# A fused attention and gated MLP: token blocks of 768, 1024 and 512 in place of three of 768

## The chip, the cores and the metric

The kernel runs on one core of a Trainium2 chip. What counts is the time of one execution on the device, in microseconds, as the median of three runs.

## What is computed

Attention with a causal mask and a memory term, over 4 batches, 8 heads, 576 positions and head size 64, gives x of 2304 tokens by 512. A gated MLP follows, which is where the change lies:

```python
g = x @ w_gate            # 512 -> 1536
silu = g * (1.0 / (1.0 + np.exp(-g)))
val = x @ w_val
return silu * val @ w_out # 1536 -> 512
```

All of it is float32. A product in the MLP is made of three matmuls on operands that are split into a high and a low part (names ending in h and l): high x high, high x low, low x high.

## The kernel before

**Stages.** The attention runs first, up to about 183 us of the trace, and writes x to DRAM as xdh and xdl (high and low). The MLP then works on three blocks of tokens, which start at ORDER. d_ff is cut into 12 slices (f) of 128.

**Block 1** (tokens 0 to 767) goes slice by slice. For each slice its weights are decoded and split (third, operands), the up products made, and u, the gated product of 384-token halves, is multiplied with w_out at once into six PSUM banks (lower). The first three slices are plain (eight); from slice 3 on a slice is seven steps in the manner of Strassen (seven, chain), p1, p2, p6, p7, p5, p4, p3, numbered 0 to 6 here. Each step is six matmuls (product: two halves of the contraction, three of the high-low products), with a weight part of 128x128 stationary and N2 = 384 tokens moving. Steps alternate between two PSUM banks, so a bank must be read before the step after the next. Steps 2, 4, 5 and 6 add onto what their bank holds, after it has been read. After step 0 ACT copies to zp, after step 1 DVE adds it into zg, after 2 and 3 ACT copies to zh and zv, after 4 and 5 DVE adds to zv and zh, and after 6 DVE multiplies twice (use): zg and zh are then the two halves of u.

**Blocks 2 and 3** are computed only up to u, which goes to DRAM (udr) with its sums (mixed, tiles zs). During slices 6 to 11 of block 1 DVE makes the sums of x that the steps of blocks 2 and 3 need (sums, tiles xr, xt, xm for block 2 and yr, yt, ym for block 3), and ACT and DVE split them into the places of the strip xall or, for block 3, into tiles yp1h, yp1l and so on (high, low, spreads). After block 1 come solo passes: slice 11 of block 2, slice 10 of block 2, slice 10 of block 3, slice 11 of block 3. Then a paired loop takes slices 0 to 9, a step of block 2 and a step of block 3 in turn, each with its own two banks.

**The down phase** multiplies u with w_out, again in seven products, each over three chunks of d_ff for block 2 and then three for block 3 (chunks, 42 in all). A chunk has 128-token row tiles, six matmuls each, with 256 columns of w_out moving. Its operand is loaded six chunks ahead and split three chunks ahead (prep, LEAD). taken evacuates a finished product, and the last store ends the kernel.

**What sets the order.** Work on PE, ACT, DVE and GpSimd (POOL) goes out in the order in which the program text issues it (queued, whose line 92 is the line of nearly all rows). The lists plan[n] say what DVE and ACT do behind step n. An instruction waits in its queue for what it needs, and all that stands behind it on its engine waits too. Loads and stores are issued on SP's queue.

Lines that matter below: N2 and ORDER (27, 30), sums (773), product (809), chain (887), the plans of slices 6 to 11 (1002 to 1027), the solo passes (1045, 1073, 1085, 1110), the paired loop (1162), prep (1125), and the down phase (1199 to 1255).

## Time and profile before

| | |
|---|---|
| median of 3 runs | 590.47 us (589.98 to 590.79) |
| profiled execution, its own time | 590.32 us |
| span from the first to the last instruction in it | 588.5 us |
| PE busy | 579.0 us, 98% |
| DVE, ACT, POOL busy | 478.1, 391.9, 236.5 us |
| granted TensorE clock, mean | 0.997 |

The span is what lies between the first and the last instruction of the profiled execution; the 1.8 us beside it are around the program. A row of the timeline begins with the start in us from the span's start and the duration in us, then engine, line, operation, output <- inputs, sizes and how many such instructions were merged; brackets show the engine's idle time before it and what ended that. Matmuls are pipelined: a row of 0.34 us doesn't mean that the next starts after 0.34 us, so the distance between starts is what one costs. s and tr are PSUM banks, woh and wol the split down weights, th, tl, bh, bl the split up weights.

### The profile page before, as it was taken

What the parts mean: (1) busy time and instruction counts of PE and PEld (TensorE: products, weight loads), DVE (VectorE), ACT (ScalarE), POOL (GpSimd) and SP (SyncE); (2) the same over time, 40 slices, a digit from 0 to 9 for tenths busy, and PEclk for the clock granted to TensorE, in tenths of its full rate; (3) what the DMA queues carried; (4) which work ended last, traced back from release to release, by engine and by line L of the source; (5) the groups of instructions that cost most, each with busy time, mean ns of one, the idle gap of its engine ahead of it and who ended that gap; (6) DMA issues with size and microseconds to landing.
All of it is one profiled execution on the core that took longest, in us unless ns stands there. A gap on an engine that the chain in (4) does not pass through costs nothing.

```text
span 588.5 us, 11998 instructions
## 1 busy us (share of the span) xinstructions
PE 579.0 (98%) x4118; PEld 535.5 (91%) x4118; DVE 478.1 (81%) x1161; ACT 391.9 (67%) x895; POOL 236.5 (40%) x285
## 2 busy tenths in 40 slices
PE   6999999999999999999999999999999999999997
PEld 4888888878878999999999999999999999999997
DVE  7899999999988989899998778677777776985771
ACT  7898998998887578777844655444444446646741
POOL 6999999999975333433340002122220000000000
PEclk9999999999999999999999999999999999999999
DMA  8446856757417555699848587365475426998852
GB/s 252 144 141 189 282 157 200 251 170 219 171 64 278 200 176 187 209 311 280 267 163 301 163 284 224 135 215 189 178 249 215 138 111 201 310 402 279 266 194 80
DMA packets 66092, 124.26 MB, mean 211 GB/s; under 512 B 8304, under 2 KB 37360, under 8 KB 66032
## 3 DMA queue, kind: packets, MB, share of 16 engines
q1 hardware_dynamic: 65744, 123.21, 63.0%
q8 instruction: 32, 0.52, 0.4%
q10 hardware_dynamic: 288, 0.30, 0.1%
q14 instruction: 28, 0.23, 0.1%
HBM read 80.23 MB, written 43.25 MB: 210 GB/s over the span
## 4 chain that ended last, share of the span: by engine, by line
PE 94%; ACT 2%; DMA 1%; DVE 1%; POOL 1%; issue 0%; SPq 0%; ACTq 0%
PE s L92 62%; PE tr L92 32%; DMA qr<-in_qt_dram 1%; DMA up<-zh 1%; DVE xall L92 1%; POOL ps L92 0%; ACT g L92 0%; ACT ps L92 0%; POOL kl L92 0%; ACT L92 0%; DVE zg L92 0%; DVE zh L92 0%; ACT we L92 0%; ACT xall L92 0%; SPq L289 0%
## 5 line engine op out<-in xcount | busy, mean ns | idle before, releaser
L92 PE MATMUL s<-xall,th 128*128 128x384 f32 x336 | 85.8, 337 | 0.0
L92 PEld LDWEIGHTS s<-xall,th 128*128 128x128 f32 x336 | 61.0, 188 | 3.8 <-ACT zp L92 0.9
L92 PE MATMUL s<-xall,bh 128*128 128x384 f32 x252 | 64.2, 336 | 0.0
L92 PE MATMUL s<-xall,tl 128*128 128x384 f32 x168 | 56.5, 336 | 0.0
L92 POOL TENSOR_SCALAR pl<-pl,rs,og 128x384 f32<-128x384 f32 (+1 forms) x64 | 54.2, 861 | 4.8 <-DVE rs L92 4.2
L92 POOL TENSOR_SCALAR we<-we 128x512 f32<-128x512 f32 x32 | 25.2, 788 | 73.8 <-ACT we L92 70.4
L92 POOL TENSOR_TENSOR tq<-w 128x256 f32<-128x256 f32 x12 | 8.6, 740 | 108.9 <-DVE zs L92 99.2
L92 ACT ACTIVATE zh<-zh 128x384 f32<-128x384 f32 x33 | 17.3, 526 | 51.1 <-DVE zh L92 51.0
L92 DVE TENSOR_TENSOR xall<-ur,xall 128x768 fp32r<-128x768 f32 x42 | 39.3, 952 | 13.6 <-ACT xall L92 13.6
L92 PE MATMUL tr<-g,vp 128*64 128x320 f32 (+4 forms) x448 | 48.8, 360 | 0.2 <-ACT g L92 0.2
L92 PEld LDWEIGHTS s<-xall,bh 128*128 128x128 f32 x252 | 45.7, 188 | 1.8 <-DVE zv L92 0.2
L92 PEld LDWEIGHTS tr<-g,vp 128*64 128x64 f32 x448 | 29.4, 137 | 18.0 <-issue 2.7
L92 ACT ACTIVATE pl<-pl,mx 128x384 f32<-128x384 f32 (+1 forms) x64 | 42.5, 665 | 4.1 <-DVE mx L92 3.3
L92 PE MATMUL s<-xall,bl 128*128 128x384 f32 x126 | 42.3, 336 | 0.0
L92 ACT CAST xall<-ur 128x768 fp32r<-128x768 f32 x42 | 34.3, 833 | 10.2 <-PE tr L92 3.1
L92 PE MATMUL s<-kh,qh 64*128 64x128 f32 (+4 forms) x160 | 36.1, 378 | 5.0 <-ACT kh L92 4.1
L92 DVE CUSTOM_DVE_ANT_0 pl<-s,maskp 128x384 f32<-128x384 f32 (+1 forms) x64 | 38.2, 617 | 0.7 <-PE s L92 0.3
L92 ACT COPY g<-tr 128x384 f32<-128x384 f32 (+1 forms) x60 | 30.0, 526 | 4.3 <-PE tr L92 4.2
L92 ACT ACTIVATE ps<-ps,mx 128x128 f32<-128x128 f32 (+1 forms) x64 | 28.6, 454 | 6.2 <-DVE mx L92 6.0
L92 POOL TENSOR_SCALAR ps<-ps,rs,og 128x128 f32<-128x128 f32 (+1 forms) x64 | 32.0, 517 | 1.4 <-DVE rs L92 1.4
L92 PEld LDWEIGHTS s<-xall,tl 128*128 128x128 f32 x168 | 31.6, 188 | 0.0
L92 ACT ACTIVATE zg<-zg 128x384 f32<-128x384 f32 x33 | 17.3, 525 | 20.8 <-DVE zg L92 20.4
(231 smaller groups left out, 1914.7 us busy)
## 6 DMA issues: line engine op xcount, KB each, us to landing
ur<-up SPq DMA_DIRECT2D x42, 384.0 KB, 4.7
up<-zg SPq DMA_DIRECT2D x36, 192.0 KB, 2.3
wraw<-in_wg_dram SPq DMA_DIRECT2D x12, 512.0 KB, 4.0
wraw<-in_wv_dram SPq DMA_DIRECT2D x12, 512.0 KB, 4.3
wraw<-in_wo_dram SPq DMA_DIRECT2D x12, 512.0 KB, 5.1
qr<-in_qt_dram SPq DMA_DIRECT2D x15, 384.0 KB, 3.1
vp<-in_v_dram SPq DMA_DIRECT2D x16, 320.0 KB, 4.9
wr<-wdr SPq DMA_DIRECT2D x10, 512.0 KB, 3.7
```

The lines of the kernel that those rows point to most:

```text
L92: ins = getattr(eng, name)(*args, **kw)
```

## The change

Block 2 becomes tokens 768 to 1791, block 3 1792 to 2303. An up product of block 2 moves 512 columns, one of block 3 256, in place of 384 each. The down phase has four row tiles per chunk for block 2 and two for block 3, in place of three each. Since block 2's operands no longer fit into the strip, those of p4 and p3 go into the tiles that held plain weights of the first slices (halves_of), and the order in which the sums are split into their places is changed (p3 first). The small tiles zp and zv come from one pool for both blocks; pt has three buffers for four; the sums' reciprocals in the attention share one tile. The last evacuation is split between ACT and DVE, and its second store is issued on ACT's queue. The core of the diff:

```diff
N2 = 384
+NB = (512, 256)
...
-ORDER = (0, 768, 1536)
+ORDER = (0, 768, 1792)
...
-EDGE_A, EDGE_B, EDGE_X = 16, 176, 40
+EDGE_A, EDGE_B, EDGE_X = 16, 176, 24
...
+    hp = ctx.enter_context(tc.tile_pool(name="hp", bufs=1))
+    halves_of = [[hp.tile([128, 1088], F32R, name=f"wg{part}{n}") for part in "hl"] for n in range(2)]
...
-    udr = {(b, k): dram.tile([128, NF // 2, N2], F32, name=f"u{k}{b}") for k in STEPS for b in range(2)}
+    udr = {(b, k): dram.tile([128, NF // 2, NB[b]], F32, name=f"u{k}{b}") for k in STEPS for b in range(2)}
...
+    xs = places(STEPS, N2)
+    xb = places(("p1", "p2", "p6", "p7", "p5"), NB[0])
+    for p, pair in zip(("p4", "p3"), halves_of):
+        xb[p] = [two_rows(x, 16, NB[0]) for x in pair]
...
-    def sums(t0, pool_, name, here=False):
+    def sums(t0, pool_, name, w, most, here=False):
...
-    def product(ps, w, x, start):
+    def product(ps, w, x, start, n2):
...
-        pt = rot(tmp, "pt", [128, 512], F32, 4)
+        pt = rot(tmp, "pt", [128, 512], F32, 3)
...
-    hold = lambda name: rot(zwp, name, [128, N2], F32, 1 if name == "zv" else 2)
+    hold = lambda name: rot(zwp, name, [128, 512], F32, 2)
...
-                begin, due, mix = sums(ORDER[1], tmp, "x")
+                begin, due, mix = sums(ORDER[1], tmp, "x", NB[0], 512)
...
-            begin3, due3, mix3 = sums(ORDER[2], xr3p, "y")
+            begin3, due3, mix3 = sums(ORDER[2], xr3p, "y", NB[1], NB[1])
...
-            plan[3] += spreads(mix, ("h", "p6"))
-            plan[4] += spreads(mix, ("l", "p6"), ("h", "p7"))
-            plan[6] += spreads(mix, ("l", "p7"))
+            plan[2] += spreads(mix, ("h", "p3"), xs=xb)
+            plan[3] += spreads(mix, ("l", "p3"), xs=xb)
+            plan[4] += spreads(mix, ("h", "p6"), xs=xb)
+            plan[5] += spreads(mix, ("l", "p6"), xs=xb)
+            plan[6] += spreads(mix, ("h", "p7"), xs=xb)
             arrive = [
-                (1, spreads(mix, ("h", "p5"))), (2, spreads(mix, ("l", "p5"))),
-                (3, spreads(mix, ("h", "p3"))), (4, spreads(mix, ("l", "p3"))),
+                (0, spreads(mix, ("l", "p7"), xs=xb)),
+                (1, spreads(mix, ("h", "p5"), xs=xb)), (2, spreads(mix, ("l", "p5"), xs=xb)),
             ]
...
-    seven(ready[LATE[1]], xs, ring2, stored(0, LATE[1]), [], plan, (), holds(0))
+    seven(ready[LATE[1]], xb, ring2, stored(0, LATE[1]), [], plan, (), holds(0), NB[0])
...
-    seven(ready[LATE[1]], x3, ring3, stored(1, LATE[1]), [], plan, (0, 2, 4), holds(1))
+    seven(ready[LATE[1]], x3, ring3, stored(1, LATE[1]), [], plan, (0, 2, 4), holds(1), NB[1])
...
-            raw_u[n] = rot(p3a, "ur", [128, 2, N2], F32, U_AHEAD)
+            raw_u[n] = rot(p3a, f"ur{b}", [128, 2, NB[b]], F32, U_AHEAD // 2)
...
-            ops[n] = h, l = split_in[n % len(split_in)]
+            b = chunks[n][1]
+            ops[n] = h, l = split_in[b][(n // 6 * NC + n % NC) % slots_b[b]]
...
-        chains = [chain(w, xs, ring2, stored(0, f), holds(0)), chain(w, x3, ring3, stored(1, f), holds(1))]
+        chains = [chain(w, xb, ring2, stored(0, f), holds(0), NB[0]), chain(w, x3, ring3, stored(1, f), holds(1), NB[1])]
...
-    areas = [(banks[4:6], banks[6:8]), (banks[0:2], banks[2:4])]
+    areas = [(banks[4:6], banks[6:8]), (banks[0:1], banks[1:2])]
...
+            if (k, b) == chunks[-1][:2]:
+                act.mul(o[:, 0:256], ps[:, 0:256], W_ONE)
+                dve.tensor_scalar(o[:, 256:512], ps[:, 256:512], W_ONE, None, op0=ALU.mult)
+                out_to(b, i, h, o, ts[:1])
+                out_to(b, i, h, o, ts[1:], ACT)
+                return
...
-        for t in range(3):
-            ps = (a[:, 0:256], a[:, 256:512], z[:, 0:256])[t]
+        for t in range(NB[b] // 128):
+            ps = areas[b][SIDE[k]][t // 2][:, t % 2 * 256 : t % 2 * 256 + 256]
```

DVE's queue in slice 10 of block 1, from the sum xt to the addition zv, which frees the bank for step 6 (wa, wol, tt, bl and tl are weight parts). Before:

```order
L92 TENSOR_TENSOR xt_2601<-xr_2600 128x768
L92 SCALAR_TENSOR_TENSOR wa_1467<-we_1174,wa_1467 128x512
L92 TENSOR_TENSOR tt_2798<-wr_2576,tt_2798 128x256
L92 TENSOR_TENSOR bl_2802<-wr_2576,bh_2801 128x512
L92 TENSOR_TENSOR wol_2699<-wa_1467,woh_2698 128x512
L92 TENSOR_TENSOR tl_2800<-tt_2798,th_2799 128x512
L92 TENSOR_TENSOR tt_2798<-wr_2576,tt_2798 128x256
L92 TENSOR_TENSOR xm_2602<-xt_2601,xr_2600 128x768
L92 TENSOR_TENSOR zv_2920<-s_167,zv_2920 128x384
```

and now:

```order
L96 TENSOR_TENSOR xt_2599<-xr_2598 128x1024
L96 SCALAR_TENSOR_TENSOR wa_1467<-we_1174,wa_1467 128x512
L96 TENSOR_TENSOR tt_2796<-wr_2574,tt_2796 128x256
L96 TENSOR_TENSOR bl_2800<-wr_2574,bh_2799 128x512
L96 TENSOR_TENSOR wol_2697<-wa_1467,woh_2696 128x512
L96 TENSOR_TENSOR tl_2798<-tt_2796,th_2797 128x512
L96 TENSOR_TENSOR tt_2796<-wr_2574,tt_2796 128x256
L96 TENSOR_TENSOR xm_2600<-xt_2599,xr_2598 128x1024
L96 TENSOR_TENSOR zv_3028<-s_175,zv_3028 128x384
```

The order is the same; the two sums of block 2 have grown where they stood.

DVE's queue where slice 10 of block 2 ends and slice 10 of block 3, the first solo pass over it, begins (yp3l is the low part of block 3's last operand, zs a sum for the store; the row zg that reads a bank and zp is the addition behind step 1 of block 3). Before:

```order
L92 SCALAR_TENSOR_TENSOR zg_3999<-s_168,zg_3999 128x384
L92 SCALAR_TENSOR_TENSOR zh_4000<-zvw_4001,zh_4000 128x384
L92 TENSOR_TENSOR yp3l<-yr_3460,yp3h 128x768
L92 TENSOR_TENSOR zs_4062<-zg_3999,zh_4000 128x384
L92 TENSOR_TENSOR zg_4067<-s_175,zpw_4066 128x384
```

and now:

```order
L96 SCALAR_TENSOR_TENSOR zg_3997<-s_176,zg_3997 128x512
L96 SCALAR_TENSOR_TENSOR zh_3998<-zv_2918,zh_3998 128x512
L96 TENSOR_TENSOR yp3l<-yr_3459,yp3h 128x512
L96 TENSOR_TENSOR zs_4059<-zg_3997,zh_3998 128x512
L96 TENSOR_TENSOR zg_4063<-s_183,zp_3027 128x256
```

Again only the sizes differ: four operations stand ahead of block 3's first addition as before.

## Rows read from the trace of the kernel before

**Rows 1.** The page's busy time, share of the span and instructions of each engine.
```profile
PE 579.0 (98%) x4118; PEld 535.5 (91%) x4118; DVE 478.1 (81%) x1161; ACT 391.9 (67%) x895; POOL 236.5 (40%) x285
```

**Rows 2.** Chain that ended last, in order of time: start us, us, piece.
```profile
331.46 166.62 PE s L92 x960
...
511.78 6.12 PE tr L92 x54
```

**Rows 3.** Timeline of PE, down products of block 1: start us, us, instruction.
```profile
199.50 0.39 PE L92 MATMUL tr<-woh,uh 128*128 128x512 f32 x1
...
200.88 0.34 PE L92 MATMUL s<-xall,wgh 128*128 128x384 f32 x1
```

**Rows 4.** Busy time by stretch: PE, PEld, DVE, ACT, POOL, clock, DMA share, GB/s.
```profile
262.50:308.20 45.70, 45.70 (x241) 42.12 (x240) 43.52 (x78) 32.40 (x64) 17.11 (x15) 1.00 0.76 242
346.20:498.90 152.70, 152.70 (x883) 152.70 (x882) 108.40 (x213) 72.47 (x152) 19.47 (x24) 1.00 0.56 187
```

**Rows 5.** Timeline of DVE, end of slice 9 of block 1.
```profile
295.01 0.68 DVE L92 TENSOR_TENSOR tl<-tt,th 128x512 fp32r<-128x512 f32 x1
295.61 1.39 DVE L92 TENSOR_TENSOR xr<-xr,xt 128x768 f32<-128x768 f32 x1
296.92 0.55 DVE L92 SCALAR_TENSOR_TENSOR zg<-s,zg 128x384 f32<-128x384 f32 x1
```

**Rows 6.** Timeline of ACT, slice 9 to 10, first and last of four in a row.
```profile
297.50 0.51 ACT L92 CAST uh<-zg 128x384 fp32r<-128x384 f32 x1 [1.85 <-DVE zg L92]
...
298.96 0.46 ACT L92 COPY zp<-s 128x384 f32<-128x384 f32 x1
```

**Rows 7.** Timeline of PE, slice 10: first products of steps 2 and 6.
```profile
299.51 0.57 PE L92 MATMUL s<-xall,th 128*128 128x384 f32 x2
...
306.48 0.53 PE L92 MATMUL s<-xall,bh 128*128 128x384 f32 x2
```

**Rows 8.** Timeline of DVE, slice 10.
```profile
300.52 1.40 DVE L92 TENSOR_TENSOR xt<-xr 128x768 f32<-128x768 f32 x1
...
304.93 0.95 DVE L92 TENSOR_TENSOR xm<-xt,xr 128x768 f32<-128x768 f32 x1
305.80 0.55 DVE L92 TENSOR_TENSOR zv<-s,zv 128x384 f32<-128x384 f32 x1
```

**Rows 9.** Timeline of DVE, start of block 3's first solo pass, first and last of five.
```profile
338.80 0.56 DVE L92 SCALAR_TENSOR_TENSOR zg<-s,zg 128x384 f32<-128x384 f32 x1
...
341.11 0.56 DVE L92 TENSOR_TENSOR zg<-s,zpw 128x384 f32<-128x384 f32 x1
```

**Rows 10.** Timeline of PE, the same pass: steps 0, 1 and 3 begin.
```profile
338.60 0.34 PE L92 MATMUL s<-yp1h,bh 128*128 128x384 f32 x1
...
339.64 0.34 PE L92 MATMUL s<-yp2h,bh 128*128 128x384 f32 x1
...
340.14 0.34 PE L92 MATMUL s<-yp2h,bl 128*128 128x384 f32 x1
...
341.88 0.34 PE L92 MATMUL s<-yp7h,th 128*128 128x384 f32 x1
```

**Rows 11.** Timeline of ACT, the same pass.
```profile
342.50 0.60 ACT L92 ACTIVATE pt<-tr 128x512 f32<-128x512 f32 x1
```

**Rows 12.** Timeline of DVE, down phase: operands of the sixth and seventh chunk.
```profile
508.68 0.95 DVE L92 TENSOR_TENSOR xall<-ur,xall 128x768 fp32r<-128x768 f32 x1
...
510.61 0.95 DVE L92 TENSOR_TENSOR xall<-ur,xall 128x768 fp32r<-128x768 f32 x1
```

**Rows 13.** Timeline of PE: the down phase's first product, and around the sixth chunk.
```profile
498.94 0.28 PE L92 MATMUL tr<-t0h,xall 128*128 128x256 f32 x1
...
509.27 0.28 PE L92 MATMUL s<-t0l,xall 128*128 128x256 f32 x1
509.68 0.50 PE L92 MATMUL s<-t0h,xall 128*128 128x256 f32 x2
...
510.02 0.29 PE L92 MATMUL s<-t0l,xall 128*128 128x256 f32 x1
```

**Rows 14.** Timeline of ACT: the last two evacuations, 512 and 256 columns.
```profile
584.58 1.06 ACT L92 ACTIVATE oc<-s 128x512 f32<-128x512 f32 x2 [5.05 <-PE s L92]
```

More of the change, by code (lines that the diff above doesn't have):

```diff
@@ L2 @@
 from contextlib import ExitStack, contextmanager
+from itertools import count
 import concourse.bass as bass
@@ L254, in third_word @@
             if j == 0:
-                held[f] = [rot(wp, f"wg{part}", [128, 1024], F32R, 2) for part in "hl"]
+                held[f] = [x[:, 0:1024] for x in halves_of[f % 2]]
             oh, ol = (x[:, c] for x in held[f])
@@ L781, in load @@
         def load(n):
-            for dst, src in ((got[:, n], xdh), (two[n % 2], xdl)):
-                ld = SP.dma_start(dst, block(src, t0, *AT[n]))
+            for dst, src in ((got[n], xdh), (two[n % 2], xdl)):
+                ld = SP.dma_start(dst, block(src, t0, *AT[n], w))
                 follow(ld, last[DVE], "the loads that come before go first", mybir.DependencyClass.Sync)
@@ L815, in product @@
                 pe.matmul(
-                    ps[:, 0:N2], wt[:, c], xx[:, kk, :], start=(start and n == 0), stop=(n == 5), skip_group_check=not start,
+                    ps[:, 0:n2], wt[:, c], xx[:, kk, :], start=(start and n == 0), stop=(n == 5), skip_group_check=not start,
                 )
@@ L885, in eight, with chain @@
         return u
-    def chain(w, x, bank, use, hold=hold):
-        p1, g1, g2, v2 = hold("zp"), hold("zg"), hold("zh"), hold("zv")
+    def chain(w, x, bank, use, hold=hold, n2=N2):
+        p1, g1, g2, v2 = (hold(name)[:, 0:n2] for name in ("zp", "zg", "zh", "zv"))
         def step(n):
@@ L893, in step @@
             ps = bank()
[L894 to L895 removed]
+            product(ps, w[p], x[p], n in (0, 1, 3), n2)
+            ps = ps[:, 0:n2]
             if n == 0:
@@ L914, in chain, with seven @@
         return step
-    def seven(w, x, bank, use, down, plan, away_at, hold=hold):
-        step = chain(w, x, bank, use, hold)
+    def seven(w, x, bank, use, down, plan, away_at, hold=hold, n2=N2):
+        step = chain(w, x, bank, use, hold, n2)
         for n in range(7):
@@ L950, in mixed @@
         a11, a21, a12, a22 = (kept_u.pop((b, f // 2 * 2 + j, i)) for j in range(2) for i in range(2))
-        s3, s2 = (rot(z2p, f"zs{n}{b}", [128, N2], F32, 1) for n in range(2))
+        s3, s2 = (rot(z2p, f"zs{n}{b}", [128, NB[b]], F32, 1) for n in range(2))
         s4 = a11 if f % 2 else a12
@@ L964, in attention_moe @@
     for p, i, j in (("p1", 0, 0), ("p2", 0, 1), ("p7", 1, 0), ("p4", 1, 1)):
-        direct(xs, first, p, i, j)
-    spreads = lambda mix, *what: [
-        (high if kind == "h" else low)(mix, p, k) for kind, p in what for k in range(2)
+        direct(xs, first, p, i, j, N2)
+    spreads = lambda mix, *what, xs=xs: [
+        (high if kind == "h" else low)(mix, p, k, xs) for kind, p in what for k in range(2)
     ]
@@ L988, in attention_moe @@
             if f == 0:
-                _, due, mix = sums(first, tmp, "x", True)
+                _, due, mix = sums(first, tmp, "x", N2, 512, True)
                 for k, some_ in enumerate(((0,), (1,), (2, 4), (3,))):
@@ L1050, in attention_moe @@
     x3p.tile([128, 16], F32, name="edge2")
-    x3 = {p: [x3p.tile([128, 2, N2], F32R, name=f"y{p}{part}") for part in "hl"] for p in STEPS}
+    x3 = {p: [x3p.tile([128, 2, NB[1]], F32R, name=f"y{p}{part}") for part in "hl"] for p in STEPS}
     x3p.tile([128, 48], F32, name="edge3")
@@ L1114, in attention_moe @@
     chunks = [(k, b, c) for k in KS for b in range(2) for c in range(NC)]
-    split_in = [xsplit[p] for p in STEPS]
+    slots_b = (3, 4)
+    split_in, at = [], 16
+    for w, n in zip(NB, slots_b):
+        split_in.append([[two_rows(strip, at + (2 * i + j) * 2 * w, w) for j in range(2)] for i in range(n)])
+        at += n * 4 * w
+    assert at <= 28 * N2 + 16
     ops, raw_u, raw_t, tset = {}, {}, {}, {}
@@ L1216, in taken @@
     def taken(k, b):
-        a, c = areas[b][SIDE[k]]
-        parts = [(a[:, 0:512], slice(0, 512), (0, 1)), (c[:, 0:256], slice(512, 768), (2,))]
+        parts = [
+            (ps[:, 0:512], slice(n * 512, n * 512 + 512), (2 * n, 2 * n + 1)) for n, ps in enumerate(areas[b][SIDE[k]])
+        ]
         if k in ("p1", "p6", "p7"):
```

65 lines of the change are left out of this document (32 added, 33 removed).

## The prediction

> **What bounds the kernel now.** First the page: TensorE (PE) is busy 98% of the span, VectorE (DVE) and ScalarE (ACT) much less [rows 1]. So the stages are read for two things: how far one matmul start lies from the next, and where PE stood still. The chain in order of time gives the first. From the first solo pass after the weights are done to the down phase it is one PE piece of 166.62 us with 960 products of 384 columns, 0.1736 us each; without a wait of 0.16 us in it (below) 0.1734. A stretch of 54 down products of 256 columns takes 6.12 us, 0.1133 each [rows 2]. Moving 512 columns appears before only in the down products of block 1: six starts in 1.38 us, 0.230 each [rows 3]; another six took 1.37, so I use 0.229. The stages differ in what stands behind PE: from 262.5 to 308.2 us DVE is busy 43.5 of 45.7 us, in the paired loop 108.4 of 152.7 [rows 4]. In the first stage anything longer on DVE can reach PE; in the second it has room.
>
> **Part 1, the up products.** Every pair of products of 384 columns (0.3468 us) becomes one of 512 and one of 256 columns (0.229 + 0.1133 = 0.3423 us). There are 12 slices of d_ff, 7 steps, 6 products: 504 pairs. 504 x 0.0045 = **2.3 us less**. Neither size has been seen in an up product, so the price is bounded: with 512 columns at twice the 256-column step (0.2267) the gain is 504 x 0.0068 = 3.4 us; with both sizes in proportion to the 384-column step it is nothing. I take the rows of the sizes themselves, being nearest. The number of columns is the same; the gain is all in what a product costs over its columns.
>
> The Trainium skill (TensorE: Matmul & The Clock Gate, Back-to-back issue gap) gives a warm gap of N/2.4 + 2.5 ns, linear in N. By that rule the pair keeps its price and part 1 is worth nothing; the rows here are not on one such line (0.1133, 0.1734 and 0.229 us rise by 0.060 and then by 0.056 per 128 columns), and that is why the rule is a rival and not the forecast.
>
> **Part 2, wider sums while block 1 still runs.** Block 2's operand sums, written to xr, xt and xm, grow from 768 to 1024 elements per partition, with nothing moved on DVE there. An operation of 512 took 0.68 us and one of 768 took 0.95 [rows 5, 8]: 0.27 us per 256 elements. In each of the slices 6 to 9 one such sum stands between DVE's reading of step 5 and that of step 6: xr, 1.39 us, then zg; ACT's casts of zg and zh, a weight piece, and only then ACT's copy zp, which frees the bank for the next slice's step 2 [rows 5, 6]. zp ends at 299.42; PE starts step 2 at 299.51, and its first two products take 0.57 us in place of 0.51 [rows 7]. The slack is nil, and the loop closes on itself: steps 2 to 5, DVE's zh, tl, xr, zg, ACT, step 2. So 0.27 us more on xr is 0.27 us more per slice, four times: **1.1 us**. xr runs beside a GpSimd operation and is longer than its size explains; were all of it to grow in proportion (1.39 x 256/768 = 0.46), it would be 1.9 us. I take 0.27, because xm of the same size takes 0.95 when alone [rows 8].
>
> In slice 10 xt and xm both stand ahead of zv [rows 8], and zv ends at 306.35, PE's step 6 starts at 306.48 and is 0.02 us late already [rows 7]: 2 x 0.27 = **0.5 us**. Behind it xr's 0.27 more and yr's 0.27 less (block 3's sums shrink to 512) cancel before the ul operations. In slice 11 the reordered spreads (p3 first, into the old weight tiles) fall where DVE has idle time, and the first pass over block 2, with steps of 6 x 0.229 = 1.37 us in place of 1.04, has more room than before: nothing.
>
> **Part 3, the first solo pass over block 3.** Its steps shrink to 6 x 0.1133 = 0.68 us. DVE's queue there, after the last step of block 2's pass: zg, zh (stores), yp3l, one zs sum, and then the sum zg that frees the bank for step 3. Before, it began 0.20 us after the pass did and the last one ended at 341.67, 3.07 us after the start at 338.60; step 3 was due, and started, at 341.88 [rows 9, 10]. Now zg, zh and zs have 512 elements (a further 0.13 each), yp3l has 512 in place of 768 (-0.27), the freeing sum 256 (-0.14): 3.05 us, the same. But step 3 is due after 3 x 0.68 = 2.04 us. Allowing 0.06 from DVE's end to PE's start, PE stands still for **1.07 us**. What is late next: ACT's zh and zv copies, held by pt evacuations of 0.60 us [rows 11] and in the second solo pass by weight casts, against steps of 0.68; I put 0.1 on each of four bank reuses, 0.4 us, at least 0 and at most 0.8. The 0.16 us at 339.64 to 340.14 (products at 0.17 would take 0.34 us, not 0.50) goes, since the smaller loads have 2.3 us longer to land [rows 10]. Part 3: **1.3 us**.
>
> **Part 4, the loop and the down phase.** In the loop a wide step follows a narrow one; between a step and the reuse of its bank lie 2.7 us (block 2) or 3.4 us (block 3) where there were 3.1, with a DVE idle for 44 of 153 us [rows 4]: nothing, and if that cover failed, 0.1 us per slice would be 1 us. The down phase has the same 756 products. PE lost 0.41 us there: the operand of the sixth chunk ended at 509.63, after PE had come to it at 509.38 [rows 12, 13]. With chunks of 24, 24, 24, 12, 12, 12 products that chunk is due at 10.88 us after the start in place of 10.2, and DVE's work ahead of it adds up to the same (wider preparations of block 2, narrower ones and sums of block 3): that wait goes. The seventh operand, 1024 wide, ends 12.6 us after the start, as it did [rows 12, 13], against a chunk due at 12.24: about 0.4 us comes back. Sum: **0**. At the end the evacuation of 256 columns by ACT, the shorter of two that take 1.06 us together [rows 14], becomes one of the same size by DVE, with the last store on ACT's queue: 0, give or take 0.2.
>
> **The sum.** -2.3 + 1.1 + 0.5 + 1.3 + 0 = +0.6 us. The profiled execution took 590.32 us, so 590.9; it stands 0.15 us under the median of 590.47, within the spread of the runs (0.8 us), so I add nothing.
>
> **Rivals.**
> *The waits are mostly covered.* If DVE's queue has slack that the rows hide (a sum starting sooner, a step 3 that isn't held), only half of the 2.9 us of new waits comes and the gain of part 1 shows: 590.32 - 2.3 + 1.4 = 589.4, and with 512 columns at 0.2267 it is 588.3. For it: a third of part 3 rests on work of ACT that the rows of before show only at the wider steps, and xr's wait is taken from durations of other operations. Against: the zp copy and zv end within 0.15 us of the step that waits for them [rows 6 to 8].
> *No gain per column (slower).* Place: the loop's and the solo passes' up products. If 512 columns cost 0.231 (4/3 of 0.1734) and 256 columns 0.1156, part 1 is nothing, and the waits stand: 590.32 + 2.9 = 593.2; with half of the waits 591.8. It decides from a pair price of 0.3457 upward, where under 0.6 us is gained. The linear gap of the Trainium skill (TensorE: Matmul & The Clock Gate, Back-to-back issue gap) would make it so. For it: neither size was seen with these operands. Against: both rows are below that.
> *The wide chunks starve the down phase.* ACT and DVE must prepare three operands of 1024 during block 3's 4.1 us. 3 x (0.95 + 0.27) + a weight part of 0.68 is 4.3 us of DVE; the lead of three chunks should carry it. Were it not to, 0.2 us in each of six rounds: 592.1.
>
> **Chances.** About 0.2% (1.2 us) is what a measurement of this kernel can tell from no change: 589.3 to 591.7. My forecast (590.9, own range 589.6 to 592.0) has 0.55, the covered waits 0.23, no gain per column 0.15, the starved down phase 0.07. Of the forecast's share I put 0.04 below 589.3 and 0.08 above 591.7; of the covered case 0.18 below and 0.05 within; of the third all but 0.02 above; of the last 0.03 within: faster 0.22, same 0.53, slower 0.25. The range reaches from 588.8 (covered waits) to 592.3 (half of the no-gain case).
>
> **What would show it.** Right: 512-column up products 0.227 to 0.231 us apart and 256-column ones 0.113 to 0.114; step 2 of slices 7 to 10 late by 0.3 us each, step 6 of slice 10 by 0.5; one gap of 1 us before the fourth step of block 3's first solo pass; no gap at the sixth chunk of the down phase. Wrong: PE gaps in the loop, a chunk of the down phase waiting in every round, or products of 256 columns further apart than 0.115.

## The result, and the profile after

The changed kernel takes **595.13 us** in the median of seven runs (592.65 to 597.65), the kernel before 590.77 beside it (589.98 to 591.48). The ratio is 1.0073, 95% interval 1.0049 to 1.0096: slower by 4.4 us. The forecast was 590.9 and its range ended at 592.3. Two things are to be explained, for the profiled execution, 592.65 us, is the fastest of the seven: why that one is 2.3 us over the kernel before, and why the others are up to 5 us above it.

PE is as busy as before [rows 1], in a span 2.3 us longer. The page's busy times of the changed kernel:

```profile
PE 579.9 (98%) x4118; PEld 512.6 (87%) x4118; DVE 477.8 (81%) x1159; ACT 387.6 (66%) x891; POOL 235.7 (40%) x285
```

From the first product of each stage to that of the next, in the two profiled executions (us):

| stage | before | changed | difference | forecast |
|---|---|---|---|---|
| start to block 1's slice 7 | 262.37 | 261.83 | -0.5 | 0 |
| block 1's slices 7 to 11 | 57.53 | 59.15 | +1.6 | +1.6 |
| block 2's two passes | 18.70 | 23.83 | +5.1 | +4.7 |
| block 3's two passes | 14.74 | 11.64 | -3.1 | -3.75 |
| paired loop | 145.60 | 143.75 | -1.85 | -1.9 |
| down phase, to its last product | 86.00 | 86.65 | +0.65 | 0 |
| last product to the end | 3.58 | 4.01 | +0.4 | 0 |

The forecast column splits part 1's 2.3 us by stage (84 wide products cost 4.7 us more in block 2's passes, 84 narrow ones 5.05 less in block 3's) and adds the waits of parts 2 and 3.

**The price of the columns is as forecast.** Timeline of PE in the loop, changed kernel (start us, us, instruction): six products of 512 columns take 1.37 us (0.229 each), six of 256 take 0.68 (0.1133).

```profile
399.59 0.62 PE L96 MATMUL s<-xall,bh 128*128 128x512 f32 x2
...
400.96 0.28 PE L96 MATMUL s<-yp1h,bh 128*128 128x256 f32 x1
...
401.64 0.62 PE L96 MATMUL s<-xall,bh 128*128 128x512 f32 x2
```

**The sums of part 2.** Timelines of DVE, of ACT and of PE, changed kernel, where slice 7 ends and slice 8 begins. xr takes 1.65 us (1.39 before, [rows 5]); zg waits for it, ACT's uh for zg, zp comes last and ends at 276.50, and PE's step 2 starts at 276.55, 0.11 us after it was due; its second product is late by as much again (0.61 us for two products, where 0.51 is usual); 0.10 us more is lost in step 1. Slices 7 to 10 lose 0.32 us each, where they lost 0.06, and slice 10's step 6 loses 0.55 (0.02 before) to the wider xt and xm.

```profile
272.42 1.65 DVE L96 TENSOR_TENSOR xr<-xr,xt 128x1024 f32<-128x1024 f32 x1
274.00 0.55 DVE L96 SCALAR_TENSOR_TENSOR zg<-s,zg 128x384 f32<-128x384 f32 x1
```

```profile
274.58 0.52 ACT L96 CAST uh<-zg 128x384 fp32r<-128x384 f32 x1 [2.11 <-DVE zg L96]
...
276.03 0.47 ACT L96 COPY zp<-s 128x384 f32<-128x384 f32 x1
```

```profile
276.21 0.42 PE L96 MATMUL s<-woh,ul 128*128 128x512 f32 x1
276.55 0.61 PE L96 MATMUL s<-xall,th 128*128 128x384 f32 x2
```

**Block 3's first pass**, timelines of PE and of DVE. The step due at 347.01 starts at 347.90; what it waits for is the sum zg, behind yp3l and zs, as [rows 9] let expect.

```profile
344.81 0.28 PE L96 MATMUL s<-yp1h,bh 128*128 128x256 f32 x1
...
347.90 0.38 PE L96 MATMUL s<-yp7h,th 128*128 128x256 f32 x1 [0.72 <-DVE zg L96]
```

```profile
346.22 0.68 DVE L96 TENSOR_TENSOR yp3l<-yr,yp3h 128x512 fp32r<-128x512 f32 x1
346.82 0.69 DVE L96 TENSOR_TENSOR zs<-zg,zh 128x512 f32<-128x512 f32 x1
347.43 0.42 DVE L96 TENSOR_TENSOR zg<-s,zp 128x256 f32<-128x256 f32 x1
```

**The down phase**, which begins at 500.20: timelines of DVE and of PE. DVE's first wide operand starts 0.75 us after the phase did (before it started with it, 498.94 both), since ACT makes the last Silus and a cast of 1024 elements first; so the sixth and the seventh operand are both late, by 0.50 and 0.56 us with the product after each, where one was late by 0.41 [rows 12, 13].

```profile
500.95 1.23 DVE L96 TENSOR_TENSOR xall<-ur,xall 128x1024 fp32r<-128x1024 f32 x1 [1.61 <-ACT xall L96]
...
510.96 0.68 DVE L96 TENSOR_TENSOR xall<-ur,xall 128x512 fp32r<-128x512 f32 x1
...
512.36 1.22 DVE L96 TENSOR_TENSOR xall<-ur,xall 128x1024 fp32r<-128x1024 f32 x1
```

```profile
511.70 0.50 PE L96 MATMUL s<-t0h,xall 128*128 128x256 f32 x2 [0.23 <-DVE xall L96]
...
513.63 0.50 PE L96 MATMUL tr<-t1h,xall 128*128 128x256 f32 x2 [0.29 <-DVE xall L96]
```

**The end**, timeline of all engines: DVE's half of the last evacuation starts when ACT's half has ended, not beside it [rows 14].

```profile
587.16 0.38 ACT L96 ACTIVATE oc<-s 128x256 f32<-128x256 f32 x1 [3.48 <-PE s L96]
...
587.58 0.42 DVE L96 TENSOR_SCALAR oc<-s 128x256 f32<-128x256 f32 x1 [9.64 <-ACT oc L96]
588.04 0.35 ACTq L1230 DMA_DIRECT2D out_dram<-oc  x1
```

The 0.5 us in the first row of the table is no part of the change. The granted clock between 10 and 20 us was 0.83 in the profiled execution before and 1.00 in this one, and the program is the same there. A second trace of the kernel before, with 1.00 as well, came to slice 7 at 261.78 us, as the changed kernel did (261.83). In the twenty traces the clock lay between 0.66 and 1.00, and the same down product of the first slice started between 195.3 and 197.7 us: at 196.8 to 197.7 in the four with a clock under 0.7, but once at 197.2 with 1.00, so the clock isn't all of it.

One thing the forecast's list did not hold: from 322.4 us until block 3 began, every product of 512 columns but one started 0.2333 us after the last one (timeline of PE, changed kernel), and those of 256 columns in block 3's passes mostly 0.1177 us.

```profile
344.11 0.40 PE L96 MATMUL s<-wgh,bh 128*128 128x512 f32 x1
344.35 0.40 PE L96 MATMUL s<-wgl,bh 128*128 128x512 f32 x1
344.58 0.40 PE L96 MATMUL s<-wgh,bl 128*128 128x512 f32 x1
344.81 0.28 PE L96 MATMUL s<-yp1h,bh 128*128 128x256 f32 x1
```

So each size has **two paces**, 0.0043 us apart. With 420 pairs in the loop and 756 products in the down phase, the wider one would cost 1.85 us for either size in the loop and 3.3 us below. This is the suspicion that the experiments test, beside the single waits.

### The profile page after: what moved, and what is told of

Same layout as the page of the kernel before. It is cut to its first block, busy times and chain, and to the rows that moved or that the text cites. A ratio compares the mean times of both kernels' runs of the same rounds, so it can differ in the third digit from the quotient of the medians.

```text
span 590.9 us, 11977 instructions
## 1 busy us (share of the span) xinstructions
PE 579.9 (98%) x4118; PEld 512.6 (87%) x4118; DVE 477.8 (81%) x1159; ACT 387.6 (66%) x891; POOL 235.7 (40%) x285
## 4 chain that ended last, share of the span: by engine, by line
PE 88%; DVE 6%; ACT 2%; DMA 1%; issue 1%; POOL 1%; SPq 0%; DVEq 0%; ACTq 0%; POOLq 0%
PE s L96 55%; PE tr L96 33%; DVE zg L96 1%; DVE xall L96 1%; DMA qr<-in_qt_dram 1%; DMA wraw<-in_wg_dram 1%; DVE zs L96 0%; DVE zh L96 0%; ACT xall L96 0%; ACT g L96 0%; ACT zh L96 0%; DVE xt L96 0%; DVE xr L96 0%; ACT t0h L96 0%; POOL ql L96 0%
## 5 line engine op out<-in xcount | busy, mean ns | idle before, releaser
L96 PE MATMUL s<-xall,th 128*128 128x384 f32 (+1 forms) x288 | 81.7, 365 | 0.0
L96 PE MATMUL s<-xall,bh 128*128 128x384 f32 (+1 forms) x204 | 57.9, 365 | 0.3 <-DVE zv L96 0.3
L96 PE MATMUL s<-xall,tl 128*128 128x384 f32 (+1 forms) x144 | 52.6, 365 | 0.0
L96 ACT ACTIVATE zh<-zh 128x512 f32<-128x512 f32 (+2 forms) x33 | 17.2, 525 | 53.6 <-DVE zh L96 53.6
L96 DVE TENSOR_TENSOR xall<-ur,xall 128x1024 fp32r<-128x1024 f32 (+1 forms) x42 | 39.0, 951 | 12.9 <-ACT xall L96 12.9
L96 ACT CAST xall<-ur 128x1024 fp32r<-128x1024 f32 (+1 forms) x42 | 34.1, 834 | 13.6 <-DMA ur<-up 6.6
L96 PE MATMUL s<-xall,bl 128*128 128x384 f32 (+1 forms) x102 | 37.1, 363 | 0.0
L96 DVE TENSOR_TENSOR zv<-s,zv 128x512 f32<-128x512 f32 (+2 forms) x33 | 18.2, 555 | 22.2 <-PE s L96 19.4
L96 DVE TENSOR_TENSOR zg<-s,zp 128x512 f32<-128x512 f32 (+2 forms) x33 | 18.3, 554 | 19.5 <-PE s L96 12.8
L96 PE MATMUL tr<-t0h,xall 128*128 128x256 f32 x192 | 33.3, 276 | 0.0
```

The source lines that it names most:

```text
L96: ins = getattr(eng, name)(*args, **kw)
```

## Experiments

**The same kernel again.**

> The changed kernel once more, for a second trace and more times: its seven times lie between 592.65 and 597.65 us, and the trace shows the fastest. Theory A (a pace that the matmuls keep): between 322.4 and 357 us of that trace the 512-column products start 0.2333 us apart and the 256-column ones 0.1177, elsewhere 0.229 and 0.1133, and the pace changes only where PE stood still; PE never stands still in the loop, so a run that enters it at the wide pace keeps that for 420 pairs of 0.0087 us, 3.7 us. Then the times fall into groups some 3.7 us apart (near 592.7 and 596.3, with the stalls' own spread about them), and a trace over 595 us has a loop of 147.4 us in place of 143.75. Theory B (the waits vary): the paces in the loop are 0.229 and 0.1133 in every trace, and a slower trace has longer PE gaps at slices 6 to 10, the solo passes or the start of the down phase. Theory C (the clock at the start): a granted clock below 1.0 within the first 30 us costs a slower trace some us there, and nothing else differs.

Seven times from 593.81 to 600.86 us, median 595.72 (ratio 1.0092, 1.0059 to 1.0125). The trace is of the run at 593.81: loop 143.73 us, down phase 86.66, the same gaps, block 2's passes now at 0.229. It differs by its start, with one of the two lowest clocks of the study there (stretch of 10 us: busy times, granted clock, DMA share, GB/s):

```profile
10.00:20.00 10.00, 8.07 (x46) 6.74 (x46) 5.81 (x26) 8.23 (x25) 9.60 (x15) 0.66 0.60 194
```

This start was 1.4 us later than in the profiled run above: theory C holds for some of the spread, in both kernels. It can't be all of it: the highest time, 600.86 us, came at a mean granted clock of 1.000, as did 592.65 and 596.33 above. For the rest no trace of a higher time was taken.

**Block 2's sums one place later.**

```
-            plan[5].append(due[5 - left])
+            plan[6].append(due[5 - left])
...
-            plan[5].append(due[3])
+            plan[6].append(due[3])
...
-            for k, work in zip((1, 3, 5), due[4:]):
+            for k, work in zip((1, 4, 6), due[4:]):
```

> The changed kernel with block 2's sums one place later in DVE's order: the four additions into xr behind the last step's products zg and zh (where each stood ahead of them), xm behind zv, the last xr behind zg and zh. Theory (part 2 of the prediction): these sums held zg and with it ACT's zp copy and zv, so the PE gaps of slices 6 to 10 (1.28 us at step 1 and step 2 of four slices, 0.55 at step 6 of slice 10) go, all but 0.2 us, and the stage from the first product of slice 7 to that of slice 11 takes 45.6 us in place of 47.5 or so; the whole is 1.5 us shorter than the changed kernel, about 591.2 beside its best 592.65. Rival (the DVE queue as a whole is too full there): the additions come out of the same time, the ul operations behind them are late in their place, and the gaps move to the down products of step 2 with at least half their size, 1 us.

Worse: 597.01 us (595.49 to 598.57). Slices 7 to 9 take 12.2 us each in place of 11.73. The rival was right, and the timelines of DVE and PE say how: without xr DVE stands still 0.54 us until the last step is done, xr comes behind, and ul is late by more than zp was.

```profile
275.67 0.56 DVE L96 SCALAR_TENSOR_TENSOR zg<-s,zg 128x384 f32<-128x384 f32 x1 [0.54 <-PE s L96]
...
277.21 1.22 DVE L96 TENSOR_TENSOR xr<-xr,xt 128x1024 f32<-128x1024 f32 x1
278.34 0.97 DVE L96 TENSOR_TENSOR ul<-zg,uh 128x384 fp32r<-128x384 f32 x1
```

```profile
279.37 0.51 PE L96 MATMUL s<-woh,ul 128*128 128x512 f32 x1 [0.51 <-DVE ul L96]
```

**The freeing sum first in block 3's pass.** yp3l moves from the pass before into step 2, the zs sums from steps 0, 1, 2, 4 to 1, 2, 3, 4.

> The changed kernel with two operations moved on DVE in the first pass over block 3 alone: the sum zg that frees the bank for the fourth step comes ahead of the zs sum and of yp3l, which now come behind it. Theory (part 3 of the prediction): PE's gap of 0.89 us before the fourth step goes, all but 0.1 us; the small gaps (0.9 us in all) stay. The two passes over block 3 take 10.8 us in place of 11.64, and the whole is 0.9 us shorter than the changed kernel. Rival (ACT's copies hold the banks next): the gap moves to the next steps and less than 0.4 us is won. By the theory of the two paces the solo passes of block 2 still run at 0.2333 us, since their pace was set by a gap earlier.

595.14 us (593.93 to 596.53). The gap of 0.89 us goes and one of 0.48 comes before the seventh step, where zv now stands behind the four moved operations; the two passes take 11.15 us in place of 11.64. The rival was nearer. But this trace (594.96 us) holds the find of the study. Its PE gaps at the start of the down phase are those of the profiled run above (0.50 and 0.56 us), and behind them every product to the end starts 0.1177 us after the last. Chain in time, here and then in the first trace of the changed kernel (start, us, piece):

```profile
521.57 4.24 PE s L96 x36
525.81 8.48 PE tr L96 x72
```

```profile
521.85 4.08 PE s L96 x36
525.93 8.16 PE tr L96 x72
```

The phase takes 89.50 us in place of 86.65 at a granted clock of 1.00, with no other wait.

**The down phase and the tail mended.**

```
-                dve.tensor_scalar(o[:, 256:512], ps[:, 256:512], W_ONE, None, op0=ALU.mult)
+                o2 = rot(p3b, "oc", [128, 1024], F32, 3)
+                dve.tensor_scalar(o2[:, 256:512], ps[:, 256:512], W_ONE, None, op0=ALU.mult)
...
-                out_to(b, i, h, o, ts[1:], ACT)
+                out_to(b, i, h, o2, ts[1:], ACT)
...
-        some_sums(2)
+        some_sums(1)
```

> The changed kernel with one pending sum of block 2 or 3 ahead of each chunk of the down phase in place of two, and with the last 256 columns of the output evacuated by DVE into a tile of its own. Theory on the tail: DVE's last operation began only when ACT's into the same tile had ended (587.16 to 587.54, then 587.58), so with another tile both run together and the end comes 0.4 us earlier after the last product (3.5 us in place of 3.93). Rival: both read the same PSUM bank and still go one after the other; nothing is won. Theory on the chunks: the sixth and seventh operands were late (PE gaps 0.50 and 0.56 us) because eight sums stood ahead of them on DVE; with three of them behind, 3 x 0.41 us, both gaps go, 1.0 us. Rival: the operands wait for the loads of the stored sums; the gaps stay or move to a later chunk.

Both gaps go: the phase takes 85.57 us, 1.08 less. The tail does not move (4.01 us): with a tile of its own DVE still waits for ACT. That leaves the PSUM bank that both read as the likeliest reason.

```profile
586.08 0.38 ACT L96 ACTIVATE oc<-s 128x256 f32<-128x256 f32 x1 [3.48 <-PE s L96]
...
586.50 0.42 DVE L96 TENSOR_SCALAR oc<-s 128x256 f32<-128x256 f32 x1 [9.64 <-ACT oc L96]
```

The Trainium skill (PSUM — Partial Sum Buffer, PSUM bank collisions raise a hardware error) says that the compiler orders any two engines that touch one bank in the same partitions, reads among them; the rows agree. Ten times lie at 591.57 to 594.30 (seven) and at 598.97, 599.63 and 599.81: two groups 5 to 8 us apart. Without a gap in the down phase the pace of the loop may go on to the end: 3.65 + 3.3 us.

**The sums in halves, where DVE waits anyway.** Each of the four additions becomes two of 512 elements, in steps 3 and 5; in slice 10 xm moves behind zv, and xr's last step into slice 11.

> The changed kernel with block 2's four additions into xr done in halves of 512 elements, one ahead of zv of the slice (where DVE had 0.5 us idle) and one where the whole stood; in slice 10 xm comes behind zv and the last xr moves into slice 11. Theory (part 2, with the lesson of the run before: each of these sums was late by what it holds up, and has to stand where DVE waits anyway): xr holds zg for 0.7 us in place of 1.65, zp and zv are in time, and the PE gaps of slices 6 to 10 (1.28 + 0.55 + 0.27 us) shrink to 0.4 or less: five slices from the first product of slice 7's steps take 57.0 us in place of 59.1. Rival (DVE has no room left in these slices): 0.08 us more per slice for the second start makes the gaps grow or move; less than 0.5 us is won. The times keep their spread of several us, as the solo passes and the start of the down phase still stand still.

Of the gaps in slices 6 to 10 one is left (0.28 us at slice 7's start): part 2 was what cost 1.6 us, and where a sum stands and in what pieces decides, not its size in all. The time is 592.30 (590.94 to 597.05; ratio 1.0024, 1.0005 to 1.0043). The traced run took 593.22 all the same: PE waited 0.96 us at block 2's second step, and its loop took 145.60 us, with 512-column products at 0.229 and 256-column ones at 0.1177.

**A lighter pass over block 3.** No zs sum in it (five places per slice in the loop in place of four), yp3l in step 2, block 1's last evacuations one pass earlier.

> The changed kernel with the four zs sums of block 2 moved out of block 3's first solo pass into the loop (five places per slice in place of four), yp3l behind the freeing sum zg, and the last three evacuations of block 1 one pass earlier, into block 2's. Theory (part 3): DVE and ACT then have little but the freeing operations in the first pass over block 3, so both gaps seen so far (0.89 us before the fourth step, or 0.48 before the seventh when only the order was changed) go, and the small ones shrink: the two passes take 10.3 us or less in place of 11.64 (9.52 by their products). Rival (the steps of 0.68 us are shorter than the time from a step's end to its bank being free, whatever else is queued): some 1 us of gaps stays. In the loop PE does not wait.

The two passes take 10.57 us, 1.07 less; PE still loses 0.01 to 0.16 us at nine places. 593.19 us (591.50 to 594.76). In its trace PE stands still for 1.73 us at block 2's second step. Timelines of PE and of SP's queue:

```profile
324.80 0.50 PE L96 MATMUL s<-xall,bh 128*128 128x512 f32 x1 [1.56 <-DMA xall<-xdl]
```

```profile
315.04 0.56 SPq L267 DMA_DIRECT2D wdw<-wa  x1
315.70 1.68 SPq L780 DMA_DIRECT2D xall<-xdl  x1
```

The load of that operand's low half is the last of its queue. In the kernel before the same load was issued at 310.58 us, ahead of block 3's; with 1024 elements per operand its place in the strip now reaches into that of block 1's p6, so it has to wait for that step, and the queue was put in another order.

**All of it, and two banks for block 3's outputs.** The halved sums, the lighter pass and one sum per chunk together; block 3's areas are `(banks[0:2], banks[2:4])`, one bank per row tile.

> The changed kernel with the halved sums, the lighter solo pass, one sum per chunk in the down phase, and for block 3's outputs two PSUM banks of 256 columns each in place of one of 512, so that ACT and DVE read the last two tiles from different banks. Theory (all waits as costed): the trace ends 3.5 us after the last product in place of 3.93, and is 1.6 + 1.2 + 1.1 + 0.4 = 4.3 us shorter than the changed kernel's 592.65 less 0.35 for its wide pace in block 2's solo passes: 588.0 where the clock is full from the start, up to 2 us more where it is not. Theory A on the spread (a pace picked where PE stands still and kept until it stands still again): the last place where PE stands still is in the solo passes, so the times form two groups, 588 to 590 us and 7 us above (420 pairs at 0.0087 and 756 products at 0.0044 us), as in the run with the down phase alone mended (seven of ten at 591.6 to 594.3, three at 599.0 to 599.8). If no gap is left, one group. Rival B (the slow runs come from waits that vary): the mended waits take the slow group away or smear it between.

**589.25 us** (587.61 to 594.46, twelve runs) beside 591.09: ratio 0.9973, 0.9953 to 0.9994. This version is faster than both. The traced run took 587.85, as worked out. From the last product's start it is 3.37 us to the end: ACT's half, in a bank of its own, is read before the last product is done, and DVE's waits for PE alone. Whether the two could run side by side this doesn't show, since ACT has ended when DVE begins. Of the twelve times one lies at 594.46 and one at 592.19, the others below 590.7; a group 7 us higher is not seen. Timeline of the end:

```profile
582.32 0.39 ACT L96 ACTIVATE oc<-s 128x256 f32<-128x256 f32 x1 [2.80 <-PE s L96]
...
583.00 0.42 DVE L96 TENSOR_SCALAR oc<-s 128x256 f32<-128x256 f32 x1 [9.15 <-PE s L96]
```

**384 columns ahead of the loop.** Six products of 384 columns, result unused, in the kernel with the down phase mended.

> The kernel with the down phase alone mended, and six products of 384 columns whose result is not used ahead of the loop: 1.04 us more of PE. Theory A2 (a product of 384 columns has one pace, 0.1733 us, after every stall seen so far, and 512- and 256-column products behind some are always at 0.229 and 0.1133): the loop and the down phase then start at the narrow pace in every run, so all ten times lie within about 3 us, 592.4 to 595.5, and none 7 us higher. Rival A3 (the pace is kept through products of 384 columns, which only do not show it): three in ten lie near 600 to 601 as before. Rival B (waits vary): the spread stays, without two groups.

Five times, 595.88 to 597.57: above the 592.4 to 595.5 expected. The trace (596.79 us; its start is 1.7 us later than in the first trace of the kernel with the down phase mended) has 0.57 us of wait at the second step and, behind products of 384 columns at 0.1733, a loop of 145.60 us with 256-column products at 0.1177. Theory A2 falls: products of 384 columns do not set the narrow pace. In the down phase behind it the same size ran at 0.1133, with no stall between.

**The second step's operand in a place that is free early.** p2 goes into the old weight tiles, p4 into the strip, and p2's load is issued first.

```
-    xb = places(("p1", "p2", "p6", "p7", "p5"), NB[0])
-    for p, pair in zip(("p4", "p3"), halves_of):
+    xb = places(("p1", "p6", "p7", "p5", "p4"), NB[0])
+    for p, pair in zip(("p2", "p3"), halves_of):
...
-    for p, i, j in (("p1", 0, 0), ("p2", 0, 1), ("p4", 1, 1)):
+    for p, i, j in (("p2", 0, 1), ("p1", 0, 0), ("p4", 1, 1)):
```

> The changed kernel with one exchange of places: block 2's operand of the second step (p2) lies in the old weight tiles, which have been free since slice 2, and that of the sixth step (p4) in the strip. Theory (a transfer that the prediction did not price): with 1024 elements per operand p2's place in the strip overlaps that of block 1's p6, so its load was the last of eight in SP's queue, issued at 315.4 us, and PE waited for it at block 2's second step in every trace but one or two, by 0.03 to 1.73 us. Now that load goes early, and that gap is gone in the trace; the others stay. The two stretches of 512-column products then start behind products of 384 columns without a stall and run at 0.229 us. The whole is 0 to 1.7 us shorter than the changed kernel; the spread by the pace of the loop and the down phase (1.85, 3.65 and 3.3 us) stays. Rival (the queue is the bound, not its order): p4's load, now last, or the loads of block 3 behind it are late in its place.

The gap is gone, as the timeline of PE at the second step shows: it starts on time, from the old weight tiles, and all six follow at 0.229. Of thirteen traces with the old place two had no gap there, six one under 0.2 us and five 0.57 to 1.73. 594.01 us (591.92 to 596.31).

```profile
321.93 0.39 PE L96 MATMUL s<-xall,bl 128*128 128x512 f32 x1
322.16 0.39 PE L96 MATMUL s<-wgh,bh 128*128 128x512 f32 x1
322.39 0.39 PE L96 MATMUL s<-wgl,bh 128*128 128x512 f32 x1
```

**All of it with that exchange**, and **the same with four banks in turn.** In the second one the steps of block 3's two slices no longer add up in the two banks that they share, so its outputs for that block are other ones; the operations are the same in number and size.

> All mended waits (halved sums, lighter solo pass, one sum per chunk, two banks for block 3's outputs) and the exchange of places of p2 and p4. Theory: the gap at block 2's second step (0.19 us in the last trace, up to 1.7 in others) goes: the times' group lies at 587.4 to 589.5 us, depending on the clock of the first 20 us. The small gaps in the passes over block 3 alone stay (0.9 us), and with them the choice of a pace for the loop: where a trace or a time falls in the wide pace it is 1.85 us (256-column products alone) to 7 us (all, to the end) longer.

> The same with four PSUM banks in turn, in place of two, for the two passes over block 3 alone. Theory: the gaps there came from banks that were not free yet; with four they go, and the two passes take 9.7 us in place of 10.57 (9.52 by their products at 0.1133). Theory A on the spread: PE then stands still nowhere between block 1's slices and the end, so the narrow pace of the 384-column stage is kept: one group of times, 586.5 to 588.8 us, none 1.85 or 7 us higher. Rival B (the pace changes by itself, or is set where the size changes from 384 to 512 or 256 columns): slower times appear as often as in the kernel beside it, and a trace shows 256-column products 0.1177 us apart with no stall ahead of them.

The first: 589.11 us, eleven of its times at 587.31 to 594.10, beside 590.27 on that chip (ratio 0.9987, 0.9967 to 1.0006); the twelfth took 963.39 us at a mean granted clock of 0.56, where the eleven have 0.99 and more. The second: 588.46 (586.98 to 590.75; 0.9971, 0.9956 to 0.9985); three of its nine times lie above the 588.8 expected. Its two passes over block 3 take 9.89 us without a gap, which is 84 products at 0.1177 (stretch: PE, PEld, DVE, ACT, POOL, clock, DMA share, GB/s):

```profile
343.45:353.34 9.89, 9.89 (x85) 9.89 (x84) 7.11 (x15) 5.20 (x14) 0.00 (x0) 1.00 0.55 188
```

So the wide pace also comes without a stall, when the size changes, and leaves again (the loop behind it took 143.75 us). Theory A, as I had put it, is half wrong: pace and stall are not cause and effect. That none of nine times lies 5 us above the median, against one of eleven and one of twelve in the two versions with gaps, is too few to say more.

**The kernel before, again.**

> The kernel before once more, for a second trace: is its down phase, behind the one gap of 0.41 us at the sixth chunk, ever at 0.1177 us per product? Theory: the pace is picked at each stall, so it can be; its 40 and more times lie between 590 and 593.1 us, though, so in nearly all of them it was not. The 384-column products are 0.1733 us apart behind every stall. Rival: its down phase has only one pace, and what is new in the changed kernel is not the stall but the layout.

589.65 us; the gap at the sixth chunk is 0.30 us and 0.11 behind it, and the down phase ran at 0.1133. Whether it can run at the wider pace stays open; its times, some seventy in this study, lie between 589.40 and 593.14 us.

**Four more executions of the kernel with the down phase mended**, to catch one from the group near 599 us.

> The kernel with the down phase and the tail alone mended once more, for its trace: seven of its ten times lie at 591.6 to 594.3 us and three at 599.0 to 599.8. Theory A: a time over 598 us has a loop of 147.4 us in place of 143.75 (512-column products at 0.2333 and 256-column ones at 0.1177 us) and a down phase of 88.9 us in place of 85.57 (at 0.1177); a time under 595 us has neither, or the loop at 145.6 us. Theory B: a time over 598 us has PE gaps that the others lack, or a lower granted clock, with the products at the same pace.

> As slow_hunt_1, the same kernel in another execution: over 598 us with a loop of 147.4 and a down phase of 88.9 us, or under 595 us with 143.75 (or 145.6) and 85.57.

> As slow_hunt_1, the same kernel in a third execution: over 598 us with a loop of 147.4 and a down phase of 88.9 us, or under 595 us with 143.75 (or 145.6) and 85.57.

> As slow_hunt_1, the same kernel in a fourth execution: over 598 us with a loop of 147.4 and a down phase of 88.9 us, or under 595 us with 143.75 (or 145.6) and 85.57.

592.72, 594.78, 597.88 and 594.96 us. The chain in time of the first, the second and the third, from the fourth step of block 3's first pass (906 products of that pass, the next and the loop, then the first round of the down phase):

```profile
349.10 152.43 PE s L96 x906
501.53 8.16 PE tr L96 x72
509.69 4.08 PE s L96 x36
```

```profile
349.23 154.31 PE s L96 x906
503.54 8.18 PE tr L96 x72
511.72 4.08 PE s L96 x36
```

```profile
348.04 155.25 PE s L96 x906
503.29 8.48 PE tr L96 x72
511.77 4.24 PE s L96 x36
```

In this stretch the instructions and the gaps are the same and the granted clock is 1.00 in each. Against the first, the third loses 2.82 us in the 906 products (its loop took 146.53 us: 256 columns at 0.118, 512 at 0.2308 on average, in every slice alike, and so less than the 147.4 expected) and 7 x 0.48 = 3.36 in the down phase, and started 1.06 earlier: 5.12, and the times differ by 5.16. The second and the fourth have the loop at 145.60 us and waited 0.95 and 1.28 us at the second step. Theory A's paces, and B for the second step, account for what was seen; a time from the group above 598 us was not caught.

**Does the wait set the pace?** In the sixteen traces so far the five with over 0.5 us of wait at the second step were the five with a loop of 145.60 us. So the wait was made by hand, twice, in the kernel with the exchanged places:

```
+    late = xb["p2"][1][:, :, 0:384]
+    ins = pool.tensor_scalar(late, late.bitcast(F32), 1.0, 0.0, op0=ALU.mult, op1=ALU.add)
+    follow(ins, last[DVE], "the second step waits", mybir.DependencyClass.Sync)
     seven(ready[LATE[0]], xb, ring2, stored(0, LATE[0], True), down, plan, (3, 5, 6), hold, NB[0])
```

> The kernel with the second step's operand loaded early, and one GpSimd operation that rewrites three quarters of that operand's low half by itself, begun when DVE has finished block 1's last zh: PE then waits some 0.7 to 1.2 us before the second product of block 2's second step, as it did for the late load in five traces of sixteen. Theory D1 (that wait sets the loop's pace): the loop takes 145.6 us, its 256-column products 0.1177 us apart, in both executions. Theory D2 (wait and pace have a common cause, or none): it takes 143.75 us, as in ten of the eleven traces without that wait.

> The same kernel in a second execution: D1 a loop of 145.6 us, D2 one of 143.75 us, with a wait of 0.7 to 1.2 us at block 2's second step in both.

593.80 and 595.00 us. PE waited 0.90 us at that place in both, and the loops took 143.74 and 145.60 us. In the chain, the 828 products from the same step on (two narrow passes and the loop, short of its end), first and second run:

```profile
349.06 139.47 PE s L96 x828
```

```profile
348.61 141.12 PE s L96 x828
```

D1 falls as a rule: one program, the same wait, two paces. A link remains all the same: of the seven traces with that wait, made or not, six have the loop of 145.60 us, of the eleven without it none (one has 146.53). What picks the pace stays open.

## Why the prediction was wrong

The forecast was 0.6 us more; the profiled execution took 2.3 us more and the median 4.4. Three steps failed. Part 4, put at nothing, cost 1.1 us: DVE's first operand of the down phase begins later, and DVE's half of the last evacuation waits for ACT's. Part 3, put at 1.3 us, cost 1.95. And the sum gave products of a size one price and the load of block 2's second step none, where both differ from execution to execution; that this makes the rest of the median is argued from the variants.

**Part 1: the price was right, that it is one price was wrong.** 0.229 and 0.1133 us are what the loop shows in eleven of eighteen traces of the changed kernel and its variants, and there the loop is 1.85 us shorter, as worked out. In six the narrow products took 0.1177 (145.60 us, which is the old loop's time: the gain is gone), in one both sizes were wider. The rival "no gain per column" named 0.1156 as the bound; it came true in some runs and not in others, which no single trace could show. The Trainium skill (TensorE: Matmul & The Clock Gate, Back-to-back issue gap) has one spacing per size, set by weight load and product together; the runs here show two for a size. The rows from which I took the prices, the down products of both sizes, ran at the narrow pace in both traces of the kernel before, and its 384-column products had one pace in all traces.

**Part 2: right.** 1.62 us came where 1.6 was said, slice by slice, and went when the sums were moved to idle places.

**Part 3: mis-sized.** The large gap is as forecast (0.89 us and 0.11 for the product behind it, against 1.07), but in place of 0.4 for four late bank reuses there are ten places with 0.03 to 0.24 us each, 0.86 over the two passes; and the pace adds 0.3.

**Part 4: wrong in both halves.** "DVE's work ahead of it adds up to the same" is true, but it begins 0.75 us later, behind ACT's Silus and a wider cast; no row of DVE alone shows that. So the sixth chunk's wait, forecast to go, stayed (0.50 us), and the seventh's, forecast at 0.4, was 0.56: 1.07 us in place of 0.41. The due times 10.88 and 12.24 us are those of a chunk's first product, too, while DVE's half is first read by the third, 0.23 us later [rows 13]; by the forecast's own figures the seventh's wait would have been 0.2. "0, give or take 0.2" for the tail is +0.43: I took two engines on two halves of one PSUM bank to run side by side.

**Not on the list:** the load of block 2's second step. I had costed slice 11 at nothing, by DVE's idle time alone, and never asked which loads the wider operands' places now hold back: 0 to 1.73 us, differing from run to run.

By the table the profiled run is 2.3 us above the kernel before, and the forecast 0.6: part 3 gave 0.65, block 2's passes 0.45 (the pace, and 0.1 at the second step), part 4 1.1, the start -0.5. The median's further 2.5 us can be paces, the second step's wait and the start: the variants' traces show each of these at such sizes, but of the changed kernel itself no trace above 593.81 us was taken. The rival "chunks starve the down phase" had the right place, but two chunks wait there, the sixth and the seventh, and not one in every round.

What sets the pace stays open: not a stall alone, not products of 384 columns ahead, not the wait at the second step alone, as three experiments showed.

## What to carry over

A profile is one execution: before a price per product is multiplied by a thousand, look at several, and at the spread of the times of kernels that use the same sizes. When operands grow in a buffer that is reused in place, ask for every load which earlier reader its new place overlaps, and where that puts it in the queue. An operation that is in the way is moved to a place where its engine waits anyway, in pieces that fit there; moved just behind its victim it made this kernel slower.

## What the runs showed of the hardware that was not expected

- Products of 256 columns have two steady paces, 0.1133 and 0.1177 us, and those of 512 two, 0.229 and 0.2333, at the same granted clock of 1.00; in the loop the two sizes can be in different ones. One of them is kept over hundreds of products, and a change comes with a stall or a change of size, not with each. Products of 384 columns were at 0.1733 us in every trace.
- A delay of PE of over 0.12 us shows at two products: the one that waited starts late, and the one behind it another 0.10 to 0.12 us late, for every size seen (153 places in the MLP of the twenty traces). A delay of 0.01 to 0.115 us shows at one product alone (208 places). So the gap before the product that waited is some 0.11 us short of what was lost.
- ACT and DVE reading different columns of one PSUM bank go one after the other (587.16 and 587.58 us), with one tile or two for their results; DVE's row names ACT's as what released it.
